# Another order for the opening of an attention and gated feed-forward kernel

## The chip, the core and the metric

The kernel runs on one core of one Trainium2 chip. The metric is the device time of one execution, in microseconds (us). A core has a matrix engine (TensorE, PE in the profile, with PEld for its weight loads), VectorE (DVE), ScalarE (ACT), GpSimd (POOL), and SyncE (SP), which here only issues transfers. Each engine takes its instructions strictly in order; semaphores let one wait for another.

## What is computed

Attention within chunks of 64 tokens, and a gated feed-forward network on its output, all in fp32:

```python
scores = scale * q_c @ k_c.T              # 8 batches, 8 heads, 9 chunks of 64, head size 64
attn = softmax(scores)
x = (attn @ v_c), heads side by side      # 4608 tokens x 512
g = x @ w_gate; val = x @ w_val           # 512 x 1536 each
out = (g * sigmoid(g) * val) @ w_out      # 1536 x 512
```

## The kernel before

The 4608 tokens are nine blocks of 512. The 1536 hidden columns are twelve slices f of 128. To keep fp32's precision, both operands of a large product are split into an upper and a lower part, and three products (lower with upper, upper with lower, upper with upper) are summed. One product of 128 x 128 with 128 x 512 is one matmul instruction; a slice of `g` or `val` is twelve of them (four k, three kinds i).

The blocks 0 and 1 come first, together: a loop takes both through the slices f = 1 to 10, and prepares and saves the weights of later slices beside it; slice 11 and the other blocks follow. All that comes ahead of that loop is "the opening". In it the attention of blocks 0 and 1 is computed, each in two couples of head pairs, (block, couple) = (0,0), (0,1), (1,0), (1,1), and the first slice's products of block 0. The order of its steps on all engines is written out by hand in the string `opening`; each engine takes its own steps in that order. A step is a letter and digits: block, then head pair (S, T, C, U, L) or couple (the others), then the half h.

- S: scores of a head pair, on TensorE, into a PSUM bank. M: maxima, and K: their splitting, on VectorE. B: subtraction of the maxima by a matmul. E: exponentials, on ScalarE. Z: sums, R: inverses, on VectorE. N: multiplication of a couple by the inverses, on VectorE or GpSimd.
- T: transposes by TensorE, C: copies of them by ScalarE. X: product with the values for a couple, on TensorE. U: upper part by ScalarE, L: lower part by VectorE of a head pair's result.
- G0_ki, V0_ki: one of the twelve matmuls of `g` and of `val` of block 0 (k is the head pair, i = 0 reads L, the others U). H0: silu on ScalarE. Q0: multiplication with `val` (`times`) on VectorE.
- g, v, w1, w2 with s, b, h, j, u, l: preparation of weights (gate and value half of slice 0, slices 1 and 2), s, b, u on ScalarE, h, j, l on VectorE. e0, e1: two copies each by ScalarE, of values whose halves are exchanged; GpSimd does the same for block 1.
- .4, .6: so many transposes whose result nobody reads (`keep_warm`).

Behind the string come the same slice's products of block 1 (`pg`, `pv`, into the two PSUM banks that `g` and `val` of block 0 leave), the silu `h1`, the splitting of `h0` (`parts`) and of the output weights (`out_weights`), and the loop. In the loop, TensorE does `gate(a0, f)`, `value(a0, f)`, then the projection (`project`, L514 to L516) of the step before, and the same for `a1`.

PSUM has four banks for `ps_o`, two for `ps_a` and two for `ps_gv`; in the opening, S, T and X of the couples take those of `ps_o` and `ps_a` in turn. The loads are issued on SP in the order of the code: queries and keys, values, weights. Steps on TensorE, ScalarE and VectorE keep the order of the code; GpSimd's order is chosen by the framework's planner.

## Time and profile before

| | |
|---|---|
| median of 3 runs | 904.76 us (904.74 to 905.46) |
| the profiled execution | 905.2 us, of which its span 903.4 us |
| busy: TensorE, its weight loads | 892.7 us (99%), 739.3 us (82%) |
| busy: VectorE, ScalarE, GpSimd | 524.3 us (58%), 373.9 us (41%), 9.2 us (1%) |
[...]

The span is the time from the first to the last instruction of the profiled execution. Times within it are counted from its start. The opening is about its first 37 us, up to the first product of block 1. Busy time of TensorE includes the transposes that nobody reads.

### The profile page before, as it was taken

Reading aid. Unit: us, or ns where it says so; the run is one execution under the profiler, and the core shown is the slowest. Engines: PE = TensorE matmul, PEld = TensorE weight load, DVE = VectorE, ACT = ScalarE, POOL = GpSimd, SP = SyncE. Lnnn points to the kernel's source line nnn. Section 1 sums busy time; section 2 is a strip of 40 time slices with the busy share of each in tenths; the row PEclk is TensorE's granted clock in tenths of the full one; section 3 lists DMA queues with packets and bytes.
Section 4 is the critical chain, followed back from the end, with each engine's and each line's share of the span. In section 5 each row is a group of like instructions: output and inputs, shape, how many; then the busy total and the mean of one; then the engine's idle time right before and its main releaser. Section 6 shows DMA issues by size and latency. Waiting matters only on the chain.

```text
span 903.4 us, 14747 instructions
## 1 busy us (share of the span) xinstructions
PE 892.7 (99%) x6083; PEld 739.3 (82%) x6083; DVE 524.3 (58%) x809; ACT 373.9 (41%) x565; POOL 9.2 (1%) x13
## 2 busy tenths in 40 slices
PE   7999999999999999999999999999999999999998
PEld 6788888887888888888888888888888888888886
DVE  6876766645687655776763646766745533333332
ACT  5865555443514335424333545234325432233232
POOL 1200000000000000000000000000000000000000
PEclk9999999999999999999999999999999999999999
DMA  9499999789744456755685958665767565556651
GB/s 358 203 377 348 324 327 317 282 296 371 251 158 141 164 190 258 265 202 186 228 298 222 341 179 288 233 224 189 228 246 240 207 239 199 198 222 233 232 188 47
DMA packets 70867, 219.07 MB, mean 242 GB/s; under 512 B 30480, under 2 KB 30736, under 8 KB 55568
## 3 DMA queue, kind: packets, MB, share of 16 engines
q1 hardware_dynamic: 69360, 215.51, 66.6%
q10 hardware_dynamic: 1440, 2.62, 0.8%
q8 instruction: 48, 0.79, 0.3%
q14 instruction: 19, 0.16, 0.0%
HBM read 174.59 MB, written 43.52 MB: 241 GB/s over the span
## 4 chain that ended last, share of the span: by engine, by line
PE 97%; DMA 2%; SPq 0%; issue 0%; ACT 0%; DVE 0%
PE ps_gv L451 22%; PE ps_a L973 22%; PE ps_gv L973 16%; PE ps_o L514 11%; PE ps_o L515 11%; PE ps_o L516 11%; PE ps_a L263 2%; DMA qk_t<-in_qk 2%; PE ps_a L341 1%; PE ps_a L441 1%; PE ps_a L640 0%; PE ps_a L427 0%; SPq L235 0%; SPq L380 0%; ACT xh L590 0%
## 5 line engine op out<-in xcount | busy, mean ns | idle before, releaser
L973 PE MATMUL ps_a<-x,factors 128*128 128x512 f32 x864 | 219.2, 389 | 0.0
L973 PEld LDWEIGHTS ps_a<-x,factors 128*128 128x128 f32 x864 | 162.2, 188 | 33.7
L451 PE MATMUL ps_gv<-xh,w 128*128 128x512 f32 x576 | 176.0, 390 | 0.1
L973 PE MATMUL ps_gv<-x,factors 128*128 128x512 f32 x648 | 164.4, 389 | 0.0
L973 PEld LDWEIGHTS ps_gv<-x,factors 128*128 128x128 f32 x648 | 121.6, 188 | 25.3
L514 PE MATMUL ps_o<-both,hl 128*128 128x512 f32 x336 | 132.1, 393 | 0.5 <-DVE hl L63 0.5
L515 PE MATMUL ps_o<-both,hh 128*128 128x512 f32 x336 | 130.9, 390 | 0.0
L516 PE MATMUL ps_o<-both,hh 128*128 128x512 f32 x336 | 130.8, 389 | 0.0
L451 PEld LDWEIGHTS ps_gv<-xh,w 128*128 128x128 f32 x576 | 108.1, 188 | 22.5 <-ACT xh L590 0.2
L451 PE MATMUL ps_gv<-xl,w 128*128 128x512 f32 x288 | 110.9, 391 | 0.0
L63 DVE TENSOR_TENSOR hl<-h,hh 128x512 fp32r<-128x512 f32 x98 | 67.6, 690 | 68.4 <-ACT hh L62 68.2
L62 ACT CAST hh<-h 128x512 fp32r<-128x512 f32 x98 | 60.6, 619 | 96.5 <-PE ps_o L516 51.3
L328 DVE STREAM_TRANSPOSE turned<-s_sb 32x256 f32<-32x256 f32 x192 | 83.6, 436 | 2.7
L977 DVE TENSOR_TENSOR h<-h,ps_gv 128x512 f32<-128x512 f32 x36 | 24.7, 687 | 101.6 <-PE ps_gv L973 101.4
L514 PEld LDWEIGHTS ps_o<-both,hl 128*128 128x128 f32 x336 | 63.1, 188 | 14.7 <-DVE hl L63 0.8
L516 PEld LDWEIGHTS ps_o<-both,hh 128*128 128x128 f32 x336 | 63.1, 188 | 13.2
L515 PEld LDWEIGHTS ps_o<-both,hh 128*128 128x128 f32 x336 | 63.1, 188 | 12.7
L495 DVE SCALAR_TENSOR_TENSOR h<-v,h 128x512 f32<-128x512 f32 x72 | 49.9, 693 | 37.8 <-ACT h L1022 33.4
L1022 ACT ACTIVATE h<-ps_a 128x512 f32<-128x512 f32 x36 | 21.6, 600 | 111.7 <-PE ps_a L973 111.7
L451 PEld LDWEIGHTS ps_gv<-xl,w 128*128 128x128 f32 x288 | 54.0, 188 | 11.7 <-issue 0.2
L977 DVE TENSOR_TENSOR v<-v,ps_a 128x512 f32<-128x512 f32 x36 | 24.8, 688 | 39.3 <-PE ps_a L973 34.6
L488 ACT ACTIVATE h<-ps_gv 128x512 f32<-128x512 f32 x36 | 21.6, 600 | 62.2 <-PE ps_gv L451 62.1
(103 smaller groups left out, 861.0 us busy)
## 6 DMA issues: line engine op xcount, KB each, us to landing
factors<-w SPq DMA_DIRECT2D x36, 1024.0 KB, 4.8
factors<-t SPq DMA_DIRECT2D x36, 1024.0 KB, 6.1
both<-o SPq DMA_DIRECT2D x70, 512.0 KB, 6.3
w<-w SPq DMA_DIRECT2D x12, 1024.0 KB, 4.6
t<-th SPq DMA_DIRECT2D x12, 1024.0 KB, 8.8
two<-o SPq DMA_DIRECT2D x12, 1024.0 KB, 5.0
raw<-in_wgv SPq DMA_DIRECT2D x11, 1024.0 KB, 7.6
qk_t<-in_qk SPq DMA_DIRECT2D x10, 1024.0 KB, 6.7
```

The lines of the kernel that those rows point to most:

```text
L62: nc.scalar.copy(out=hi, in_=src)
L63: (engine or nc.vector).tensor_tensor(out=lo, in0=src, in1=hi.bitcast(F32), op=ALU.subtract)
L328: nc.vector.transpose(out=self.turned[to:to + 32, p:p + 2, j, :, 32 * (i % 2):32 * (i % 2) + 32], in_=src[32 * i:32 * i + 32, :, o // 2, 3 ...
L451: nc.tensor.matmul(ps, w, x, start=first and (k, i) == which[0], stop=last and (k, i) == which[-1])
L488: nc.scalar.activation(h, pg, AF.Silu, scale=2.0 ** -8)
L495: nc.vector.scalar_tensor_tensor(out=h, in0=pv, scalar=2.0 ** -8, in1=h, op0=ALU.mult, op1=ALU.mult)
L514: nc.tensor.matmul(o, hl[:, ts], woh, start=f == a.steps[0], stop=False)
L515: nc.tensor.matmul(o, hh[:, ts], wol, start=False, stop=False)
L516: nc.tensor.matmul(o, hh[:, ts], woh, start=False, stop=f == a.steps[1])
L973: nc.tensor.matmul(ps, w[:, u, k], x[:, v, k], start=first and k == 0 and n == 0, stop=k == NK // 2 - 1 and n == 2, skip_group_check=True)
L977: nc.vector.tensor_tensor(out=t, in0=t, in1=ps, op=ALU.add)
L1022: nc.scalar.activation(h2, ps1, AF.Silu, scale=2.0 ** -8)
```

## The change

The order of the steps in `opening` is another one. X00 of the first couple comes ahead of the scores of block 1, T02 and T03 too; X01 comes ahead of S13 and S12. The products G0, V0 begin earlier in the string but behind S13, S12, and are spread otherwise between the steps of block 1. There are 20 transposes that nobody reads, where there were 28 (besides the first 15). N00 and N11 are done by VectorE and no longer by GpSimd; N10 stays there. A new step Y0 applies silu to one column on ScalarE ahead of H0, so that the function's table is loaded there. w2s leaves the string: `up[2].scale()` comes behind `quarters.upper()`. `times(h1, pv1)` of the first slice comes ahead of `parts(a0, 0, h0)` and not in the loop's first turn. The loads and their order are the same.

```diff
--- before.py
+++ after.py
@@ -654,7 +654,7 @@
             self.a.inverse(self.z[:, :4 * T])
 
         def N(self, _):
-            self.a.scale(self.p, self.z[:, :4 * T], nc.vector if (self.a.b, self.p) == (0, 2) else nc.gpsimd)
+            self.a.scale(self.p, self.z[:, :4 * T], nc.gpsimd if (self.a.b, self.p) == (1, 0) else nc.vector)
 
         def T(self, q):
             self.a.turn_to(q, self.bank(1, [T, P])[q % 2])
@@ -683,13 +683,12 @@
 
 
     opening = """
-        gs S00 S01 .4 M001 M000 K00 gh B000 B001 .6 gb S02 S03 .6 E000 gj Z000 E001 Z001 R00 N00 M010 M011 K01
-        B010 gu e0 e1 B011 .6 E010 gl E011 Z010 vs Z011 vb T00 vh T01 .6 S11 R01 N01 S10 T02 C00 T03 C01 M100 S13
-        C03 M101 S12 K10 B100 B101 C02 vj X01 M111 E100 E101 M110 vu Z100 K11 X00 Z101 w1s U03 vl R10 B111
-        U00 U01 L03 E111 B110 G0_31 N10 V0_31 V0_02 G0_01 V0_32 E110 U02 G0_32 L01 Z110 V0_11 Z111 G0_30 L02
-        G0_11 w1b R11 V0_01 T11 L00 N11 T10 G0_10 C10 V0_10 w1h G0_21 G0_22 G0_02 V0_21 G0_12 w2s V0_22 V0_30
-        V0_20 V0_00 G0_20 V0_12 G0_00 C11 H0 T12 T13 C12 C13 X10 Q0 U11 X11 U10 U12 U13 w1j L10 L11 L12
-        L13 w1u
+        gs S00 S01 .4 M001 M000 K00 gh B000 B001 .6 gb S02 S03 .6 E000 gj Z000 E001 Z001 R00 M010 M011 K01
+        gu e0 e1 B010 B011 E010 N00 E011 T00 T01 Z010 C00 Z011 C01 .4 R01 N01 X00 vs vb gl vh T02 U00 T03 U01 S11 vj
+        L00 C02 S10 C03 L01 vu X01 S13 S12 M101 M100 K10 G0_02 G0_12 U03 M111 M110 B100 B101 K11 E100 vl U02 E101 G0_01 G0_11
+        B111 B110 Z100 Z101 R10 N10 G0_00 G0_10 E111 E110 w1s w1b Y0 Z110 Z111 R11 N11 V0_01 V0_11 V0_02
+        V0_12 V0_00 V0_10 G0_31 G0_32 G0_21 G0_22 L03 L02 T11 T10 C11 C10 V0_31 V0_32 V0_21 V0_22 T12 T13 w1h C12 C13
+        G0_30 G0_20 V0_30 V0_20 X10 H0 X11 U10 U11 L10 w1j Q0 U12 U13 L11 L12 L13 w1u
     """
     keep_warm(15)
     for do in opening.split():
@@ -703,8 +702,11 @@
             products[do[0]].add((int(do[3]), int(do[4])))
         elif do[0] == "e":
             a0.exchange(v0[int(do[1])][:, 1], values[int(do[1])][1], nc.scalar.copy)
+        elif do == "Y0":
+            h0 = hp.tile([P, N], F32, name="h")
+            nc.scalar.activation(h0[:, :1], ident[:, :1], AF.Silu)
         elif do == "H0":
-            h0 = silu(products["G"].ps)
+            nc.scalar.activation(h0, products["G"].ps, AF.Silu, scale=2.0 ** -8)
         elif do == "Q0":
             times(h0, products["V"].ps)
         else:
@@ -726,12 +728,14 @@
     o.join()
     quarters = Quarters(1)
     quarters.sums(w.t)
+    times(h1, pv1)
     p0 = parts(a0, 0, h0)
     wo_f = out_weights(0)
     lag(p0, wo_f)
     down[1].load()
     down[1].scale()
     quarters.upper()
+    up[2].scale()
 
 
     for f in range(1, NF - 1):
@@ -743,7 +747,8 @@
             quarters.save()
         down[f + 1].load()
         h0 = gate(a0, f)
-        times(h1, pv1)
+        if f > 1:
+            times(h1, pv1)
         put_off(h1)
         if f <= 2:
             quarters.lower()
```

## Rows read from the trace of the kernel before

**Rows 1.** The page, parts 1 and 4: busy time by engine, the chain's shares.

```profile
PE 892.7 (99%) x6083; PEld 739.3 (82%) x6083; DVE 524.3 (58%) x809; ACT 373.9 (41%) x565; POOL 9.2 (1%) x13
...
PE 97%; DMA 2%; SPq 0%; issue 0%; ACT 0%; DVE 0%
```

**Rows 2.** Windows: stretch, its length, each engine's busy time (instructions), clock, DMA share, GB/s.

```profile
36.90:47.90 11.00, 10.99 (x48) 9.09 (x49) 10.78 (x17) 8.49 (x13) 0.00 (x0) 1.00 0.47 168
100.00:903.00 803.00, 799.32 (x5180) 661.25 (x5178) 453.35 (x695) 313.04 (x476) 0.00 (x0) 1.00 0.66 233
```

**Rows 3.** Timeline of TensorE in the opening: start, duration, what, idle before.

```profile
14.49 0.82 PE L58 MATMUL unread<-ident 128*128 128x128 f32 x6
...
17.36 1.16 PE L263 MATMUL ps_a<-qk_t 64*64 64x64 f32 x64 [0.52 <-DMA qk_t<-in_qk]
18.56 1.06 PE L427 MATMUL ps_a<-ident,s_sb 128*128 128x128 f32 x8
...
20.99 1.13 PE L640 MATMUL ps_a<-tops,minus 128*128 128x512 f32 x4
22.05 0.57 PE L441 MATMUL ps_a<-pT,v_t 64*64 64x64 f32 x22
24.24 1.79 PE L441 MATMUL ps_a<-pT,v_t 64*64 64x64 f32 x106 [1.62 <-issue]
...
30.26 0.19 PEld L451 LDWEIGHTS ps_gv<-xl,w 128*128 128x128 f32 x1 [0.22 <-issue]
...
34.53 2.27 PE L441 MATMUL ps_a<-pT,v_t 64*64 64x64 f32 x128
```

**Rows 4.** Windows up to the stop at 22.62 and to the next at 30.25.

```profile
0.00:22.62 22.62, 17.77 (x349) 15.04 (x350) 13.82 (x29) 12.05 (x21) 2.60 (x7) 1.00 0.93 358
...
22.62:30.25 7.63, 5.93 (x128) 5.13 (x127) 6.25 (x14) 5.89 (x10) 4.72 (x5) 1.00 1.04 426
```

**Rows 5.** DMA queues in 21.9-22.1 and 27.9-28.0; then issues in 5.8-5.9.

```profile
q8 instruction: 1, 0.02, 27.5%
...
q8 instruction: 1, 0.02, 58.5%
...
raw<-in_wgv SPq DMA_DIRECT2D x1, 1024.0 KB, 16.4
```

**Rows 6.** The chain that ended last, in order of time.

```profile
5.08 14.69 DMA qk_t<-in_qk
...
36.91 11.19 PE ps_gv L451 x48
```

**Rows 7.** Timeline of GpSimd in the opening.

```profile
11.54 1.90 POOL L422 TENSOR_TENSOR s_sb<-s_sb,z 128x1024 f32<-128x1024 f32 x1 [10.23 <-DVE z L418]
```

**Rows 8.** Timeline of VectorE in the opening.

```profile
9.61 1.28 DVE L650 TENSOR_REDUCE z<-s_sb 128x8 f32<-128x512 f32 x2
...
11.13 0.25 DVE L418 RECIPROCAL z<-z 128x16 f32<-128x16 f32 x1
...
12.99 0.48 DVE L633 CAST tops<-both 128x16 fp32r<-128x16 f32 x1
...
15.17 1.28 DVE L650 TENSOR_REDUCE z<-s_sb 128x8 f32<-128x512 f32 x2 [0.89 <-ACT s_sb L644]
...
17.18 1.23 DVE L422 TENSOR_TENSOR s_sb<-s_sb,z 128x1024 f32<-128x1024 f32 x1
18.57 1.29 DVE L629 TENSOR_REDUCE both<-ps_a 128x8 f32<-128x512 f32 x2 [0.16 <-PE ps_a L263]
...
35.27 1.22 DVE L90 CUSTOM_DVE_ANT_0 t<-t 128x2048 uint16<-128x2048 uint16 x1
36.89 2.48 DVE L594 TENSOR_TENSOR xl<-ps_a,xh 128x512 fp32r<-128x512 f32 x4 [0.40 <-ACT xh L590]
```

**Rows 9.** Timeline of ScalarE in the opening.

```profile
14.54 1.09 ACT L644 ACTIVATE s_sb<-ps_a 128x512 f32<-128x512 f32 x2
...
35.78 2.06 ACT L590 CAST xh<-ps_a 128x512 fp32r<-128x512 f32 x4 [0.18 <-PE ps_a L441]
```

## The prediction

> **What bounds the kernel now.** I read the page first: the matrix engine (PE) is busy for 99% of the span and makes up 97% of the chain that ended last [rows 1]. The windows say from when on: in the 11 us that begin with the second block's first product it is busy for 10.99, and after 100 us for 799.32 of 803 [rows 2]. So what the change does to VectorE or ScalarE after the opening is hidden, and a microsecond gained or lost before about 37 us moves the end by a microsecond. The timeline of the opening comes next [rows 3]. There PE waits for transfers and softmax steps, and part of its work is filler transposes. One row stands out: the values product X01 stops after 22 of its matmuls, and PE does nothing for 1.62 us though no semaphore is waited for ("issue").

> **The change, part by part.** The loads at the start keep their order. I walk the new order with durations of rows, to the second block's first product (36.91 before, [rows 6]) and then to the first projection (48.10 before: 36.91 + 11.19).

> *Fillers.* 20 transposes instead of 28 stand in the opening. Six took 0.82 us [rows 3], so eight are worth 1.1 us, if no wait takes their place.

> *First couple at once.* The multiplication N00 leaves GpSimd (1.90, [rows 7]) for VectorE (1.23, the row of N01 at 17.18, [rows 8]) and stands behind K01. K01 ends at about 13.7 as before (12.99 + 0.48, then 0.2), so N00 ends at 14.9 and T00, T01 run from 15.0 to 16.1 (1.06 a pair, [rows 3]). ScalarE's exponentials end at 15.63 as before [rows 9], and its two copies C00, C01, about 0.52 each like the four U that took 2.06 [rows 9], at 16.65. X00 runs from 16.7 to 17.85 (half of 2.27, [rows 3]).

> *Second couple.* VectorE's sums end at 16.45 as before (15.17 + 1.28), R01 adds 0.5 (the first couple's sums end at 10.89, its R at 11.38) and N01 1.23 [rows 8]: 18.2. T02, T03 run to 19.4. Only then come S11, S10 (1.16), whose data landed at 17.3 [rows 3]: 20.55. Here the order loses: S13, S12, whose data land at 19.77, now stand behind X01.

> *The code block.* Up to X01 the new queue holds 128 instructions more for X00, 128 less for S13, S12, 8 less for B100, B101 and 16 less for the transposes. The old one reached X01 with 655 (699 less the 44 of X01), the new one does with 631. So it needs the same block 68 instructions into X01, at 20.55 + 0.6 = 21.1. When will that be there? In the old order the packet started at 21.9 and PE went on at 24.24, 2.3 later. The late packets fit one pattern: asked for while S11, S10 ran (17.36 to 18.5), with the 19.77 transfer in flight, it went out when the one after it, issued at 5.84 and landing 16.4 later at 22.2 [rows 5], was nearly done. In the new order the block before is entered one X00 earlier, near 17.0, when the transfer in flight is the one that lands at 17.3; then the packet goes out at 19.8 to 20 and the block is usable near 22.2. The row bounds this from both sides: no stop at all, or usable at 24.24 as before. I take 22.2, a stop of 1.1 us, against 1.62 + 0.22 before.

> [...]

> *Second block.* The rest of X01 takes 0.55, S13, S12 1.16: 23.9. M111, M110 (1.29, [rows 8]) and K11 (0.4) end at 25.65 on VectorE. Meanwhile PE has B100, B101 (1.13, [rows 3]) and four products of 0.23 each (11.19 for 48, [rows 6]): 25.95. B111, B110 end at 27.1, the next twelve products at 29.9. VectorE has vl (about 0.65), Z100, Z101 (1.28) and R10 (0.5) to do: 28.1; N10 on GpSimd takes 1.90 and the handover 0.16 (11.38 to 11.54, [rows 7, 8]): 30.2. So T11 waits 0.4. Then T11, T10 (1.06), four products (0.93), T12, T13, four products, and X10, X11 (2.27): 36.55. Y0 loads the silu's table while ScalarE waits for T11, and N11 on VectorE (1.23, now ahead of w1h) ends ahead of T12: both cost nothing, and some 0.5 us each if T11 came that much earlier. The sum so far is 36.55 - 36.91 = -0.35.

> *Behind X11.* U10 can run at X10's end, so L10 ends at 36.65. But w1j (1.22, [rows 8]) and Q0 (about 0.65) now stand between L10 and L11, L12, L13 (2.48 for four, [rows 8]): Q0 ends at 38.5 and L13 at 40.35. PE would reach the first product of the value bank, which Q0 frees, at 38.4, and the product that reads L13 at about 40.0: waits of 0.2 and 0.45 that the old order lacks.

> *The two moves behind the opening.* times(h1) ahead of the splits frees the value bank some 0.1 us earlier. It delays the splits by 0.7 plus a wait for the product; the projection that reads them begins after 24 more products (5.6 us), which covers it. The save of wo and the load of raw[3] behind it on SP come as much later; what waits for that load is ScalarE's scale, wanted only two steps later. up[2].scale, twice as wide as a C and so by my estimate 1.1 us of ScalarE, is moved out of the opening; ScalarE waits for TensorE on either side of it, and if that cover were gone it would cost those 1.1 us. No moved step issues a DMA.

> Sum: -0.35 + 0.65 - 0.1 = +0.2. Each handover costs some 0.05 to 0.1 that I left out, and I count one or two of these on the path: +0.3. The profiled execution took 905.2 us (span 903.4), so it becomes 905.5; the median of the runs shown, 904.76, lies 0.4 below it, so I predict 905.1 us.

> **The rivals.**
> A. *The code block is late as before, usable only at 24.24.* It happens if the request falls after 17.3, once the next transfer is in flight; my 17.0 is only 0.3 away. X01 then stops for 3.1 instead of 1.1 us, S13, S12 and all behind them come 2.0 later: 907.1. From a stop of about 2.6 us on the kernel is slower by more than 0.2%, which is 1.8 us and about what a measurement of this kernel can tell from no change.
> B. *The block is in time.* The row for it is the stop of only 0.22 at the next block [rows 3]; against it the full DMA queue until 22 us. 1.1 less: 904.0. [...] The packet at 21.9 went out 3.4 us after S11 and S10 were done (17.36 + 1.16, [rows 3]), which speaks against it.
> C. *The opening is really shorter.* As B, and VectorE keeps ahead, so that the waits before T11 (0.4) and behind X11 (0.65) vanish too: 904.0 - 1.05 = 902.9, just faster by 0.2%. Against it: these waits follow from the order on VectorE itself.
> D. *The clock falls.* PE now waits for C01, for N01 and in X01 within 7 us, with fewer fillers. The granted clock was 1.00, its higher level, throughout the old opening, with a stop of 1.62 in it [rows 4]. If it fell to half, the PE work between 22.2 and about 26 would take up to 3 us more: 908.

> **How the numbers follow.** Forecast (a stop of 0.7 to 1.6 us) 0.50, A 0.17, B 0.20, C 0.09, D 0.04. The likeliest case alone reaches from 904.6 to 905.9. For eight in ten I leave out C and D and take in B, less 0.2 for the walk's error, and A: 903.8 to 907.2. Faster by over 0.2%: C and a little of B, 0.11. Slower: A, D: 0.21. Within: 0.68.

> **What would show it.** In the profile after: an "issue" stop inside the values product that begins near 20.5, with some 699 instructions started before it, and an instruction packet 2.3 us ahead of its end; S13, S12 behind it at 22.7 to 24; T11 waiting for GpSimd's s_sb; a wait for VectorE's xl a few products behind X11; the second block's first product at 36.2 to 36.9; no change of the clock; nothing new after 50 us. The prediction is wrong in its main step if the stop is absent or ends past 23.7, if PE waits behind 50 us for the later raw load, or if the span changes by more than the first projection's start does.

## The result, and the profile after

The changed kernel takes 906.12 us (median of 22 runs, 905.07 to 906.86), the kernel before 904.62 beside it (22 runs, 903.43 to 905.46): ratio 1.0016, 95% interval 1.0010 to 1.0023. It is 1.5 us slower, which is inside the predicted range and within 0.2%, but 1.0 above the predicted 905.1 and just above the likeliest case's own range (904.6 to 905.9).

The profiled execution took 905.13 us, its span 903.3. That is one of the shortest of its 22 runs, while the profiled execution of before was 0.6 above its own median; so the two spans, 0.1 us apart, say little, and the stages have to be compared. The page, parts 1 and 4, against [rows 1]:

```profile
PE 891.4 (99%) x6075; PEld 737.7 (82%) x6075; DVE 525.4 (58%) x811; ACT 374.0 (41%) x566; POOL 5.5 (1%) x11
...
PE 97%; DMA 1%; DVE 1%; issue 0%; ACT 0%; POOLq 0%; SPq 0%; DVEq 0%
```

TensorE has eight matmuls fewer (the transposes that went) and GpSimd two steps fewer. The windows, against [rows 2]: in the 11 us from the second block's first product on TensorE is busy without a gap, and after 100 us for 799.76 of 803 (799.32 before). What the change did in this profile lies ahead of 38 us.

```profile
37.67:48.67 11.00, 11.00 (x55) 8.97 (x49) 10.79 (x18) 9.64 (x14) 0.00 (x0) 1.00 0.39 152
100.00:903.00 803.00, 799.76 (x5183) 661.97 (x5181) 454.39 (x697) 312.91 (x476) 0.00 (x0) 1.00 0.66 234
```

TensorE's timeline in the opening, against [rows 3]:

```profile
15.83 0.33 PE L441 MATMUL ps_a<-pT,v_t 64*64 64x64 f32 x4
...
18.03 1.06 PE L427 MATMUL ps_a<-ident,s_sb 128*128 128x128 f32 x8 [0.56 <-DVE s_sb L422]
19.02 1.16 PE L263 MATMUL ps_a<-qk_t 64*64 64x64 f32 x64
20.00 0.69 PE L441 MATMUL ps_a<-pT,v_t 64*64 64x64 f32 x33
22.55 0.63 PE L441 MATMUL ps_a<-pT,v_t 64*64 64x64 f32 x28 [1.85 <-issue]
...
30.73 1.09 PE L427 MATMUL ps_a<-ident,s_sb 128*128 128x128 f32 x8 [0.73 <-POOL s_sb L422]
...
34.48 1.85 PE L441 MATMUL ps_a<-pT,v_t 64*64 64x64 f32 x111
37.28 0.47 PE L441 MATMUL ps_a<-pT,v_t 64*64 64x64 f32 x17 [0.94 <-issue]
37.67 3.10 PE L451 MATMUL ps_gv<-xh,w 128*128 128x512 f32 x12
```

X00 starts at 15.83, where the old order had it behind 22 us. X01 stops after 33 matmuls for 1.85 us with no semaphore to wait for, T11 waits 0.73 for GpSimd, and a second stop of 0.94 stands in X11, where the old order had none. The second stop is a code block as well; the windows up to the first stop and from there to the second, against [rows 4]:

```profile
0.00:20.69 20.69, 15.87 (x348) 13.30 (x349) 12.75 (x25) 12.74 (x22) 0.70 (x6) 1.00 0.93 355
20.69:36.30 15.61, 13.03 (x254) 10.67 (x254) 11.14 (x23) 10.02 (x17) 4.80 (x5) 1.00 0.67 273
```

697 matmuls and weight loads up to the first (699 before), then 508. With TensorE's semaphore instructions and one drain, which the traces have and the windows don't count, it is 705 in both orders up to the first stop, and 512, twice 256, from there to the second. Both pages have 48 packets in the queue of the code (`q8 instruction: 48, 0.79`, so 16 KB each), and the traces 12,298 and 12,284 instructions of TensorE, 256 a packet. The code packets ahead of the two stops leave at 20.19 and 34.95 us. The chain of waits, against [rows 6]:

```profile
2.59 9.08 DMA v_t<-in_v
...
20.69 1.85 issue
...
36.34 0.94 issue
...
37.74 11.19 PE ps_gv L451 x48
```

The second block's first product comes at 37.74 and not at 36.91: 0.83 us later, which holds up to the first projection (48.77 against 47.94 in TensorE's timeline). And the chain no longer starts at the queries and keys of the last couple but at the values of the first block, which the new order needs early.

### The profile page after: what moved, and what is told of

Read it like the earlier page. It is cut to its first block, busy times and chain, and to the rows that moved or that the text cites. A ratio compares the mean times of both kernels' runs of the same rounds, so it can differ in the third digit from the quotient of the medians.

```text
span 903.3 us, 14731 instructions
## 1 busy us (share of the span) xinstructions
PE 891.4 (99%) x6075; PEld 737.7 (82%) x6075; DVE 525.4 (58%) x811; ACT 374.0 (41%) x566; POOL 5.5 (1%) x11
## 4 chain that ended last, share of the span: by engine, by line
PE 97%; DMA 1%; DVE 1%; issue 0%; ACT 0%; POOLq 0%; SPq 0%; DVEq 0%
PE ps_a L978 22%; PE ps_gv L451 21%; PE ps_gv L978 16%; PE ps_o L514 11%; PE ps_o L516 11%; PE ps_o L515 11%; PE ps_a L263 2%; PE ps_a L341 1%; DMA v_t<-in_v 1%; PE ps_a L441 1%; PE ps_a L427 0%; DVE z L650 0%; ACT v_t L384 0%; POOLq L1170 0%; PE pt L427 0%
## 5 line engine op out<-in xcount | busy, mean ns | idle before, releaser
L451 PEld LDWEIGHTS ps_gv<-xh,w 128*128 128x128 f32 x576 | 107.8, 188 | 22.5 <-ACT xh L590 0.2
L1013 ACT ACTIVATE h<-h 128x512 f32<-128x512 f32 x36 | 22.8, 632 | 52.9 <-DVE h L982 52.9
```

The source lines that it names most:

```text
L451: nc.tensor.matmul(ps, w, x, start=first and (k, i) == which[0], stop=last and (k, i) == which[-1])
L1013: nc.scalar.activation(h, h, AF.Silu, scale=2.0 ** -8)
```

## The experiments

Each was timed beside the kernel before, whose median was 904.33 to 904.47 us in these four sets. "First projection" is its start in TensorE's timeline: 47.94 us in the profile of before, 48.77 in that of the changed kernel.

### Without the transposes that nobody reads

The changed kernel without the 20, and the kernel before without its 28 (the first 15 stay).

```diff
-        gs S00 S01 .4 M001 M000 K00 gh B000 B001 .6 gb S02 S03 .6 E000 gj Z000 E001 Z001 R00 M010 M011 K01
+        gs S00 S01 M001 M000 K00 gh B000 B001 gb S02 S03 E000 gj Z000 E001 Z001 R00 M010 M011 K01
...
```

> The changed kernel without its 20 fillers in the opening (the first 15 stay). Theory 'code': the two stops of TensorE without a semaphore (1.85 us in X01, 0.94 us in X11) fall where its instruction stream passes multiples of 256, so 40 instructions fewer move them by 40: the first one comes after about 53 matmuls of X01 instead of 33 and ends when it did, which gives back 0.35 us; the second falls behind X11 among the large products, where 40 instructions take 4.5 us, and shrinks to under 0.3. First projection at 47.7 to 48.3 us instead of 48.94, the whole 0.6 to 1.2 us shorter than the changed kernel, about as long as the one before. Theory 'order' (the place of S13, S12 behind X01 and N10 on GpSimd cost the time): fillers stand only where TensorE waits, so within 0.3 us of the changed kernel, stops at the same matmuls. Theory 'clock': with no fillers the granted clock falls below 1.00 somewhere in 10 to 25 us, and the time grows by over 1 us.

> The kernel before without its 28 fillers in the opening. 'Code': 56 instructions fewer, so the stop comes after about 50 matmuls of X01 instead of 22 and gives back 0.45 us, and the small stop of 0.22 at 30.26 goes too: first projection at 47.4 to 47.7 instead of 48.10, the whole 0.4 to 0.7 us shorter. 'Order': within 0.3 us of before. 'Clock': granted clock under 1.00 in the opening and over 1 us longer.

Measured: 910.79 us (ratio 1.0074, 1.0060 to 1.0087) and 908.97 (1.0051, 1.0038 to 1.0065). The windows of the changed kernel without them (the figure behind GpSimd's count is the granted clock):

```profile
5.00:10.00 5.00, 2.79 (x68) 1.88 (x64) 3.15 (x7) 2.27 (x4) 0.00 (x0) 0.89 1.00 368
10.00:15.00 5.00, 3.05 (x67) 2.69 (x68) 3.83 (x9) 3.11 (x6) 0.00 (x0) 0.50 1.04 409
15.00:20.00 5.00, 4.74 (x77) 3.87 (x76) 4.13 (x8) 3.68 (x7) 0.00 (x0) 0.58 1.03 425
...
25.00:30.00 5.00, 5.00 (x85) 4.16 (x80) 2.30 (x6) 2.16 (x4) 1.40 (x3) 0.66 0.69 283
```

From 10 to 15 us the granted clock is 1.00 with the transposes (first profile of the changed kernel) and 0.50 without them. The first projection comes at 51.48. The stop in X01 comes after 53 matmuls, 20 later than with the transposes (each of them is one matmul and one weight load less ahead of the boundary), and X11 has none. The kernel before without its 28 stops behind 50 matmuls of X01, as "code" had it, but in its profiled execution, the longest of its six, for 3.36 us; its clock is 0.50 from 10 to 15 us as well, and its first projection comes at 51.58:

```profile
27.15 2.40 PE L441 MATMUL ps_a<-pT,v_t 64*64 64x64 f32 x78 [3.36 <-issue]
```

So the stop moved by as many matmuls as there were transposes fewer, 20 (33 to 53) and 28 (22 to 50). A second loss lies far away: the waits of the changed kernel without transposes begin, after 100 us, with

```profile
PE ps_a L978 <- issue: 2.6, 2, 1.4
```

two stops without a semaphore, of 1.44 us near 463 and 1.15 near 613, that the changed kernel doesn't have.

### The order of S13, S12 and X01; the place of N10

```diff
-        L00 C02 S10 C03 L01 vu X01 S13 S12 M101 M100 K10 G0_02 G0_12 U03 M111 M110 B100 B101 K11 E100 vl U02 E101 G0_01 G0_11
+        L00 C02 S10 C03 L01 vu S13 S12 X01 M101 M100 K10 G0_02 G0_12 U03 M111 M110 B100 B101 K11 E100 vl U02 E101 G0_01 G0_11
```

> The changed kernel with S13, S12 ahead of X01. 'Code': the first stop falls into S12 and ends at the same time, near 22.5; TensorE's work behind it is the same, only the wait of B111 for K11 (about 0.45) goes, since the maxima begin a microsecond earlier: 0.2 to 0.6 us shorter than the changed kernel. 'Order': S13, S12 no longer wait behind a stop in X01, the chain of the second couple starts 1 us or more earlier and all of it comes back: 0.9 to 1.5 us shorter.

Measured: 905.70 us (1.0013, 1.0005 to 1.0022). The stop is now in S12, at the same count of instructions, and X11's is where it was; the first projection comes at 48.94. "Code" was right on the place; a gain of its size or of that of "order" isn't there (the changed kernel took 906.12 and 905.79 in two sets), and the first projection is no earlier: with S13 and S12 done earlier VectorE's K11 waits 0.94 us for B100 and B101, which read the tops of K10 and still stand behind X01, and it starts at 25.72 (25.63 in the changed kernel).

```profile
21.06 0.69 PE L263 MATMUL ps_a<-qk_t 64*64 64x64 f32 x31 [0.27 <-DVE xl L594]
22.73 0.63 PE L263 MATMUL ps_a<-qk_t 64*64 64x64 f32 x28 [0.98 <-issue]
...
37.44 0.47 PE L441 MATMUL ps_a<-pT,v_t 64*64 64x64 f32 x17 [0.94 <-issue]
```

In the other kernel N10 goes to VectorE as well, so that nothing of N is left on GpSimd:

```diff
-            self.a.scale(self.p, self.z[:, :4 * T], nc.gpsimd if (self.a.b, self.p) == (1, 0) else nc.vector)
+            self.a.scale(self.p, self.z[:, :4 * T], nc.vector)
```

> The changed kernel with N10 on VectorE too, so that no multiplication is left on GpSimd. 'Code': T11's wait of 0.73 us for GpSimd goes, but Z11x, R11 and N11 come some 0.4 later on VectorE, and T12 waits instead: within 0.4 us of the changed kernel. 'Order', in the form that GpSimd's multiplication is what the change pays for: 0.7 us shorter, with no new wait ahead of T12.

Measured: 906.91 us (1.0030, 1.0018 to 1.0042). T11's wait is gone, but T12 waits 0.95 for VectorE and the first projection comes at 49.69. N10 on GpSimd isn't a cost; it relieves VectorE, whose chain sets this part.

### The two moves behind the opening alone

The step w2s leaves the string; the rest of the edit:

```diff
+    times(h1, pv1)
     p0 = parts(a0, 0, h0)
...
+    up[2].scale()
...
-        times(h1, pv1)
+        if f > 1:
+            times(h1, pv1)
```

> The kernel before with the two moves behind the opening alone: the multiplication by silu(h1) ahead of the splits, and the scale of the third weight slice out of the string and behind the upper part of the quarters. Theory 'opening' (all of the change's loss lies ahead of the first projection, 48.9 against 48.1 us): no change, within 0.3 us of the kernel before, first projection at 48.0 to 48.2. Rival 'tail' (the moves make a wait in the first turns of the loop, at the third slice's load or behind 200 us): 0.8 to 1.5 us slower, with TensorE waiting between 48 and 65 us or near 205 to 217 us.

Measured: 904.29 us beside 904.33 (1.0001, 0.9992 to 1.0010). The moves cost nothing that this run can tell, which is 0.9 us either way. This profile is also a second one of the old opening, and its stop is another:

```profile
22.43 0.57 PE L441 MATMUL ps_a<-pT,v_t 64*64 64x64 f32 x22
23.39 1.32 PE L441 MATMUL ps_a<-pT,v_t 64*64 64x64 f32 x75 [0.39 <-issue]
```

It stands behind the same 22 matmuls, but takes 0.39 us instead of 1.62. TensorE goes on 0.85 us earlier, yet the first projection comes at 47.59, only 0.35 earlier, since T11 now waits for GpSimd, which the longer stop had covered:

```profile
29.09 1.09 PE L427 MATMUL ps_a<-ident,s_sb 128*128 128x128 f32 x8 [0.57 <-POOL s_sb L422]
```

### Half as large transfers

In both kernels, the same for each of the five transfers; weight slices 1 and 2:

```diff
-            nc.sync.dma_start(out=self.raw, in_=wgv[f].rearrange("p g n -> p (g n)"))
+            pieces = 2 if f < 3 else 1
+            raw = self.raw.rearrange("p (i n) -> p i n", i=pieces)
+            src = wgv[f].rearrange("p g n -> p (g n)").rearrange("p (i n) -> p i n", i=pieces)
+            for i in range(pieces):
+                nc.sync.dma_start(out=raw[:, i], in_=src[:, i])
```

> The kernel before with five of the opening's transfers of 1 MB (both of block 1's queries and keys, weight slices 1 and 2, the output weights) issued as two of 512 KB each. Theory 'behind data' (a code packet of TensorE leaves only when the transfer in flight and the one after it are through): the packet asked for at 17.9 leaves at about 19.8 and no longer at 21.95, the stop in X01 shrinks from 1.62 to at most 0.4 us, the first projection comes at 46.8 to 47.2, and the time is 903.2 to 903.6, about 1.1 us faster. Rival 'code is slow by itself' (some 4 us from the entry into a block until the next one's packet leaves, whatever the transfers are): stop of 1.5 to 1.7 us as before, 904.5 within 0.3.

> The changed kernel with the same five transfers issued in halves. 'Behind data': the packet asked for at 16.9 leaves at about 19.0 and not at 20.2, the stop in X01 shrinks from 1.85 to 0.6 to 0.9 us, the second stop of 0.94 in X11 stays (its packet leaves after the transfers have ended), first projection at 47.7 to 48.0 in place of 48.9, time 904.9 to 905.3. 'Code is slow by itself': both stops and 906.1 as they were.

Measured: 904.14 us (0.9998, 0.9989 to 1.0007) and 905.60 (1.0012, 1.0003 to 1.0021): neither differs from its parent by more than the noise. The stops stand where they did, with 0.90 and 1.48 us:

```profile
24.08 0.64 PE L448 MATMUL ps_a<-pT,v_t 64*64 64x64 f32 x29 [0.90 <-issue]
...
22.33 0.63 PE L448 MATMUL ps_a<-pT,v_t 64*64 64x64 f32 x28 [1.48 <-issue]
```

Counting starts of matmuls and weight loads in the trace gives the moment at which TensorE enters the block ahead of the stop (256 instructions earlier). That the packet is asked for at this moment is the prediction's assumption; no trace shows the request. From there to the packet it is 3.4 us in the old order with halves (18.42 to 21.83), between the 4.1 and 2.9 of the two profiles with whole transfers; in the new order 3.0 (17.05 to 20.02) against 3.3 in the first profile and 3.0 to 3.5 in five others with whole transfers. "Behind data" falls in the form that was tested: with halves the packet doesn't leave a transfer earlier. That it waits for an amount of data already queued, however it is cut, was not tested. The profile of the new order with halves shows something else:

```profile
34.57 2.10 PE L448 MATMUL ps_a<-pT,v_t 64*64 64x64 f32 x128
36.60 3.46 PE L458 MATMUL ps_gv<-xh,w 128*128 128x512 f32 x12
```

X11 runs through, since its packet left at 33.39 and not at 34.95, and products go on 1.07 us earlier. But the first projection comes at 48.50, only 0.27 earlier, because the chain now runs over VectorE:

```profile
36.39 0.69 DVE xl L607
37.08 1.13 DVE t L90
38.21 0.60 DVE h L502
38.81 1.80 DVE xl L607 x3
...
40.66 8.00 PE ps_gv L458 x34
```

These are L10, w1j, Q0 and the other three L, the queue that the prediction named behind X11. It was there all along; the stop in X11 had covered it.

### The changed kernel once more

> The changed kernel as it is, for a second profile. If the stops belong to the order of the instructions, they stand at the same matmuls (33 into X01, 111 into X11) with 1.6 to 2.1 and 0.8 to 1.2 us, and the first projection at 48.7 to 49.2; if they are chance of one execution, they move or vanish. The time is 906.1 within 0.4. Theory 'opening' wants TensorE's waits between 205 and 217 us to differ from execution to execution without regard to the opening.

Measured: 905.79 us (1.0016, 1.0007 to 1.0025). The stops stand behind the same 33 and 111 matmuls, with 2.13 and 0.94 us. But behind the first the clock falls, which it didn't in the first profile:

```profile
21.00:23.20 2.20, 0.09 (x5) 0.01 (x1) 1.79 (x5) 0.00 (x0) 0.00 (x0) 1.00 1.05 404
...
24.20:28.00 3.80, 3.80 (x50) 3.16 (x43) 1.47 (x3) 0.97 (x3) 2.01 (x4) 0.56 1.00 412
28.00:32.00 4.00, 4.00 (x18) 3.01 (x16) 3.86 (x9) 3.99 (x7) 1.32 (x1) 1.00 0.75 312
```

In the first profile the same stretch had it at 1.00:

```profile
22.50:28.00 5.50, 5.46 (x111) 4.52 (x111) 3.56 (x7) 3.28 (x7) 2.90 (x4) 1.00 1.03 423
```

From the end of the stop to T11 it takes 9.41 us here (23.22 to 32.63) and 8.18 there (22.55 to 30.73), so this execution, at 908.06 the longest of its eleven, loses 1.2 us by the clock; the first projection comes at 50.72. Of the eleven three have a mean granted clock of 0.997 or 0.998, of the 22 above none, and of the kernel before none.

### Fewer instructions, as much work

Long matmuls in place of most transposes, alone and with S13, S12 ahead of X01:

```diff
+    def keep_warm_long(n):
+
+        ps = ps_gv.tile([P, 4, P], F32, name="unread", tag="ps_gv")
+        for _ in range(n):
+            nc.tensor.matmul(ps, ident, ident.rearrange("p (o m) -> p o m", o=1).broadcast_to([P, 4, P]), start=True, stop=True)
...
-    keep_warm(15)
+    keep_warm_long(2)
+    keep_warm(2)
```

> The changed kernel with 31 of its 35 opening transposes that nobody reads replaced: 29 by five fp32 matmuls of 128 x 512 that nobody reads either, so that TensorE is as busy with about 38 instructions fewer (19 matmuls with their weight loads). Theory 'count' (TensorE stops where the 256th instruction of a block falls): the stop in X01 comes after 52 matmuls of it and not after 33, still 1.5 to 2.1 us; X11's last 17 matmuls now lie ahead of the boundary, so its stop of 0.94 is gone, and 0.2 to 0.6 us of waits for VectorE's xl appear behind X11 in its place; first projection at 48.3 to 48.7 instead of 48.8, time 905.4 to 905.9. Rival 'burst' (X11 stops because 128 small matmuls follow each other): a stop of 0.9 in X11 as before and 906.1. If the long matmuls don't hold the clock, it falls to 0.5 in the opening and the time is above 908.

> As the one with long fillers, and with S13 and S12 ahead of X01. Theory 'count' puts the end of the block behind S12 by some 3 matmuls of X01: S13, S12 end at 21.3 to 21.6 with no stop, TensorE stops 1.5 to 2.1 us at the start of X01, and VectorE uses this time for the second block's maxima; the wait of T11 for GpSimd (0.7) and the stop in X11 (0.94) vanish, first projection at 47.3 to 48.1, time 904.2 to 905.2, about that of the kernel before. Rival 'the place of the stop doesn't matter' (what is gained behind it is lost to X01, whose results the first products need): first projection at 48.5 to 49.0, 905.6 to 906.1.

Measured: 911.16 us (1.0083, 1.0070 to 1.0096) and 909.49 (1.0066, 1.0053 to 1.0079), first projection at 51.00 and 50.94. TensorE's timeline of the first:

```profile
20.50 1.00 PE L447 MATMUL ps_a<-pT,v_t 64*64 64x64 f32 x52
24.35 0.39 PE L447 MATMUL ps_a<-pT,v_t 64*64 64x64 f32 x11 [2.86 <-issue]
...
37.09 2.10 PE L447 MATMUL ps_a<-pT,v_t 64*64 64x64 f32 x128
...
462.37 0.50 PE L987 MATMUL ps_a<-x,factors 128*128 128x512 f32 x1 [1.17 <-issue]
...
613.20 0.85 PE L987 MATMUL ps_a<-x,factors 128*128 128x512 f32 x3 [1.23 <-issue]
```

"Count" is right to the matmul (52), and X11 runs through. The size of the stop isn't: 2.86 us. The clock was granted at 1.00 up to the stop and is 0.51 from 25.5 to 29 us behind it:

```profile
20.00:24.30 4.30, 1.50 (x100) 1.36 (x92) 2.89 (x7) 0.80 (x2) 0.00 (x1) 1.00 1.03 410
...
25.50:29.00 3.50, 3.50 (x23) 2.73 (x13) 1.74 (x5) 1.13 (x3) 1.27 (x3) 0.51 0.79 322
```

And the two late stops are back, 2.4 us together: 38 matmuls and loads fewer in the opening move the boundaries of 256 behind it by as much. Counted on from the first stop in the trace of the changed kernel, in steps of 256 and 38 further, two boundaries lie ahead of the last two (457.5 us) and the last three (607.1) matmuls of a group into `ps_a`; here the stops stand ahead of the last one and the last three of such groups. The code packets leave there at 460.04 and 610.93 us, 2.3 ahead of TensorE's going on; for the two stops in the opening of the changed kernel it is 2.4 and 2.3 (20.19 to 22.55, 34.95 to 37.28). In the second kernel the boundary fell 12 matmuls short of S12's end, TensorE stopped there for 2.05 us, and the clock fell too; it can't tell what the stop's place is worth.

### Four products ahead of X01

```diff
-        L00 C02 S10 C03 L01 vu X01 S13 S12 M101 M100 K10 G0_02 G0_12 U03 M111 M110 B100 B101 K11 E100 vl U02 E101 G0_01 G0_11
+        L00 C02 S10 C03 L01 vu G0_02 G0_12 G0_01 G0_11 X01 S13 S12 M101 M100 K10 U03 M111 M110 B100 B101 K11 E100 vl U02 E101
```

> The changed kernel with four products of block 0 (G0_02, G0_12, G0_01, G0_11; 0.93 us in all) moved from behind S13, S12 to ahead of X01. Theory 'delay' (a code block is usable some 5.6 us after TensorE enters the block ahead of it, so the stop is what the instructions of that block don't fill): X01 stops after 29 matmuls, for 0.8 to 1.1 us and not 1.85, and goes on at 22.4 to 22.8 as before; S13, S12 end when they did, and the second block's chain on VectorE with them, so TensorE waits 0.7 to 0.9 us longer ahead of B111 and T11 and the first projection stays at 48.6 to 49.0: 905.5 to 906.1. Rival 'filled stop is gain': nothing takes the place of the shorter stop, first projection at 47.9 to 48.2, 904.9 to 905.2.

> As the one with four products ahead of X01, and S13, S12 between them and X01. 'Delay': the boundary falls in S12's last third, TensorE stops there for 0.5 to 0.9 us until 22.4 to 22.8, S12 ends at 23.0 to 23.3 and not 24.2, so VectorE starts the second block's maxima 0.9 us earlier, T11's wait of 0.7 for GpSimd vanishes or shrinks to 0.3, and the first projection comes at 47.6 to 48.2: 904.4 to 905.2, about as the kernel before. Rival 'X01 bounds' (what reads X01's result, now a microsecond later, is what sets the end): first projection at 48.6 or later, 905.6 or more.

Measured: 906.07 us (1.0017, 1.0008 to 1.0026) and 905.57 (1.0013, 1.0005 to 1.0022). In the first the stop shrinks to 0.37 us, and the time is that of the changed kernel: B111 now waits for VectorE's tops, T11 for GpSimd as before, X11 for code.

```profile
23.52 0.74 PE L441 MATMUL ps_a<-pT,v_t 64*64 64x64 f32 x34 [0.37 <-issue]
...
27.06 1.19 PE L640 MATMUL ps_a<-tops,minus 128*128 128x512 f32 x4 [0.74 <-DVE tops L633]
...
31.71 1.09 PE L427 MATMUL ps_a<-ident,s_sb 128*128 128x128 f32 x8 [0.70 <-POOL s_sb L422]
...
38.36 0.46 PE L441 MATMUL ps_a<-pT,v_t 64*64 64x64 f32 x17 [1.03 <-issue]
```

Its first projection comes at 49.88, later than expected, and not by the order behind X00: X00 itself, which lies ahead of the edit, starts at 17.06 instead of 15.83. ScalarE's timeline says why (e0 and e1 are its copies of values):

```profile
11.73 1.24 ACT L384 COPY v_t<-v_t 64x512 f32<-64x512 f32 x2 [1.25 <-DMA v_t<-in_v]
14.17 1.25 ACT L384 COPY v_t<-v_t 64x512 f32<-64x512 f32 x2 [1.20 <-DMA v_t<-in_v]
15.44 1.08 ACT L644 ACTIVATE s_sb<-ps_a 128x512 f32<-128x512 f32 x2
```

In this execution the second transfer of values landed 1.2 us too late for e1, which stands ahead of the exponentials on ScalarE; in the first profile of the changed kernel e1 had no wait. The old order has e0 and e1 at the same place, but there TensorE goes on to S11, whose data land at 17.3 anyway. The second kernel's profile has the same lateness, waits 1.49 us ahead of X00, and the clock is granted at 0.50 from 19.3 to 22.4 us behind that; its first projection comes at 49.55. In the other twelve profiles e1 follows e0 without a wait, so whether the lateness is chance or belongs to these two kernels isn't shown. No stop for code is left in it, but T11 still waits 0.69 for GpSimd. Its three shortest runs (904.48 to 904.52) are 1.0 us above the shortest of before (903.49); whether this order without late values equals the old one can't be said from its one disturbed profile. No version tried beats the kernel before clear of the noise.

## Why the prediction was right, and where it wasn't

**The bound** held as far as the profiles can tell. From the first projection to the end of the span it takes 854.7 to 855.5 us in three profiles of the old order and 854.5 to 855.9 in seven of the new one (those with its 35 transposes), and none of the ten has a gap of TensorE from there to 190 us. Between 190 and 230 us TensorE waits for VectorE in profiles of both orders (0.2 to 0.5 us). But near 207 us it waits for the reload of saved output weights (`both<-o`), 0.2 to 0.9 us, in four of the seven and in none of the three; whether the change brings this about isn't shown. The tail alone measured 1.0001, with the old opening.

**The stop in X01** was the main step, and its kind and place were right: predicted behind 34 matmuls, measured behind 33. Its size was off, 1.85 us in place of 1.1, which is above the forecast case (0.7 to 1.6) and below rival A (3.1): TensorE ran dry at 20.69 and not at 21.1, and the block was usable at 22.55 and not at 22.2. In the second profile it ran dry at 21.09, as walked, but the block was usable only at 23.22. What the step missed are two sizes: the time from entering the block ahead until the next one is usable, taken as 5.2 us (17.0 to 22.2), and the time that TensorE needs for the block ahead, taken as 4.1 (17.0 to 21.1). From entering the block ahead to going on behind the stop it takes 6.4, 5.1 and 5.7 us in three profiles of the old order (before, the tail alone, halves) and 5.7, 5.9 and 5.3 in three of the new (twice the changed kernel, and halves): the code comes no later. But the block ahead lasts 4.7 us in the old order, where the rest of S11 and S10, T02, T03, S13, S12, B100, B101 and 22 matmuls of X01 stand in it, with a wait for data; it lasts 3.8 in the new, where X00's end, T02, T03, S11, S10 and 33 matmuls of X01 follow each other. Among the profiles of the new order the block that passed faster had the longer stop at its end: 3.8 us and 1.85 (2.13 in the second profile, 1.48 with halves), with S13, S12 ahead of X01 4.7 and 0.98, with four products ahead of X01 5.0 and 0.37. My pattern, that the packet waits for the transfer in flight and the next one, named the right time (19.8 to 20; it left at 20.19) for a reason that the halves speak against.

**The second stop** was not predicted. The walk counted instructions up to the first boundary and went no further; two blocks on it is X11, again 128 short matmuls, and 0.94 us.

**The waits behind X11** were predicted with 0.65 and cost nothing, since VectorE worked through its queue in the second stop. Where that stop was absent they came, as the chain with halves shows, and took back 0.8 of 1.07 us.

**T11's wait** was 0.73 in place of 0.4, for GpSimd's N10 began at 28.77 and not at 28.3. With N10 on VectorE the first projection is another 0.9 later. **The transposes** were costed as time alone, eight as 1.1 us if no wait took their place. The eight were not missed in the first profile, but without all 20 the clock was granted at 0.50 from 10 to 15 us, and the first stop came 20 matmuls later.

**The sum**, along the path to the first projection: the first stop ends 0.35 later than walked, T11 starts another 0.18 later, the second stop adds 0.94, 0.28 was counted too much between them, and the 0.65 behind X11 didn't come. That makes 0.54 over the predicted +0.30, which is the measured +0.84 of the chain. That the sum came so near is partly luck: the 0.94 that was not foreseen and the 0.65 that didn't come largely cancel, though the first covers the second. Three profiles with the old opening have the first projection at 47.94, 47.59 and 47.78; the changed kernel at 48.77 and, with the clock's fall, at 50.72. So the undisturbed one is 1.0 behind the mean of the three, where the medians differ by 1.5. Three things were seen to lengthen single executions of the new order: the fall of the clock behind the longer stop (rival D, which had 4 in 100), the late values that the new order doesn't hide (in the two profiles of the kernels with four products ahead), and the wait near 207 us. The clock can hardly make up the half microsecond: 3 of 33 runs have a mean clock below 0.999, and runs with 1.000 alone spread from 904.64 to 906.86. What it is made of stays open, and so does the prediction's own sign that the span must not change by more than the first projection's start does. Two other signs failed: the second block's first product came behind 36.2 to 36.9, and the wait for xl was not seen.

**The rivals.** A (usable only at 24.24) didn't happen, nor did B and C, for the stop was longer than the row of the old order. D's half is a level that runs of this case show: 0.50 from 10 to 15 us in both kernels without the transposes; in the first profile of the changed kernel the clock stayed at 1.00. After 100 us the windows of the two kernels agree (TensorE busy for 799.32 and 799.76 of 803 us); in the opening the stops cost 0.4 to 3.4 us where short matmuls fill a block, and in three kernels with fewer instructions 1.15 to 2.04 us near 462 and 613 us as well. B had the code there in time; in the six profiles above the packets left 2.9 to 4.1 us after the entry, with whole and with half transfers.

Open besides: why X11's packet left 3.3 us after TensorE had entered the block ahead, though the transfers had ended by 32.5 us (with halves 1.6, in the old order 1.1); and why the code took longer with fewer transposes, 6.7 us with the long matmuls and 8.1 in the kernel before without its 28.

## What to carry to other kernels

Where an engine works through many short instructions and stops without a semaphore, count them from stop to stop and ask how long as many take in the new order: here the stops stood 256 instructions of TensorE apart or twice that, and a better order let the 256 ahead of the first one pass in 3.8 us instead of 4.7, with a stop of 1.48 to 2.13 us behind them in three profiles of the new order and of 0.39 to 1.62 in three of the old. Work that nobody reads may hold the clock (0.50 from 10 to 15 us without it, 1.00 with it), and instructions added or removed may move stops far behind them (1.15 to 2.04 us near 462 and 613 us with 38 to 40 fewer in the opening), so look for "issue" stops in the whole timeline, not near the edit. And bringing a step forward makes its inputs' landing times matter that the old order hid (values that landed 1.2 us too late put X00 at 17.06 and not at 15.83): take a second profile before trusting a microsecond.

## What was not expected of the hardware

The granted clock fell in the opening without any change of the instructions: with the same stream it was 0.56 for 3.8 us behind a stop of 2.13 us and 1.00 behind one of 1.85. Behind the stop of 2.86 it was 0.51 for 3.5 us; in the last kernel it was 0.50 for 3.1 us after TensorE had waited 1.49 ahead of X00 and 0.56 behind it. The length of one wait alone doesn't tell which: the kernel before kept 1.00 behind 1.62, more than that 1.49.

And 38 to 40 matmuls and loads fewer in the first 16 us (three kernels of the new order) made stops of 1.15 to 2.04 us appear near 462 and 613 us, in code that was not touched.
